# Two FFN layers behind forgetting attention: block products for w_out in the second layer's last three sets, accumulated in PSUM

## The chip, the cores and the metric

The kernel runs on one core of a Trainium2 chip. The metric is device time in microseconds (us) for one launch; "before" is the median of three runs. One further execution was recorded by the hardware profiler, and all rows below are from that one. Engines are called PE (TensorE: matmul), PEld (its weight loads, which overlap PE), DVE (VectorE), ACT (ScalarE), POOL (GpSimd) and SP (SyncE, which issues most DMAs).

## The reference, cut to what matters

```python
x = attention(q, k, v, f)                  # -> 2304 tokens x 512
for w_in, w_out, bend in ((moe_w_in, moe_w_out, lambda h: h - np.tanh(h)),
                          (moe2_w_in, moe2_w_out, lambda h: h / (1.0 + np.exp(-h)))):
    h = x @ w_in                           # 512 -> 2048
    x = bend(h) @ w_out                    # 2048 -> 512
```

The weights arrive as float64 and are decoded on the chip. Every matmul operand is kept as a high and a low float32r part, so one product of two matrices is three matmuls: high times high, high times low, low times high.

## The kernel before

The feed-forward part is cut into 24 units `u`: layer `l` (2), set `s` of 512 hidden columns (4), block `b` of 768 tokens (3). The change begins at unit 15, so layer 2 (`l` = 1), set 1, and covers units 15 to 23.

**w_in.** A set has two pairs `q` of 256 hidden columns. For each pair a slot (two slots in a unit) forms the hidden block by seven block products (`product`, line 417) in place of eight: the block of x (two halves of the 512 inputs by two halves of 384 tokens) and the block of w_in enter as sums and differences. A block product is two halves of the contraction times three terms, six matmuls of 384 columns. Each goes to a PSUM bank of its own (`ps_h`, four banks). DVE adds the banks up in SBUF (`add`, line 470), ACT applies the bend (line 447), and ACT and DVE make the high and the low part `gh`, `gl` of the bent block (lines 456 and 460). The seven sums of x, split into high and low, lie in DRAM (`xd`) and are loaded again for each unit (`xload`, line 290, 768 KB each).

**w_out.** `project` (line 385) multiplies plainly. In layer 2 the bent block is the stationary operand and w_out the moving one: a unit takes 72 matmuls of 512 columns, in 16 "halves" that a slot's list of pieces (`P1 G P6 G P2 G G P7 G P5 G P4 G P3 G`, P a product, G a half) puts between the products of the next unit. They add up in two pairs of banks (`ps_a`), and DVE adds them into `x` (line 401) or, in the last set, into `ob`, which is stored (line 405). The last half uses 256 columns (line 367).

**Weights.** A decode of one pair is: load raw (line 146), `scale` on ACT (155), `shift`, `exponent`, `low`, `join` on DVE (159, 163, 166, 174), four block sums on DVE for w_in (179), then the high part on ACT (191) and the low part on DVE (193). `fills` deals these jobs to slots; w_out is only joined and split. The scratch tiles are `wa`, `wb` and `ws`.

The whole order is written out by hand: each engine executes its instructions in program order.

Of the kernel before, what the change touches and what calls it, by code (L numbers as in the profile page):

```python
# [14 lines left out]
P = 128  # L15
# [22 lines left out]
KA = {1: 1, 2: 2, 3: 6, 4: 0, 5: 3, 6: 4, 7: 5}  # L38
# [3 lines left out]
def forgetting_attention_two_ffn(  # L42
# [16 lines left out]
    rawp = ctx.enter_context(tc.tile_pool(name="rawp", bufs=2))  # L59
# [68 lines left out]
    def open_pools(bank=None, **bufs):  # L128
        for name, n in bufs.items():
            pools[name] = ctx.enter_context(tc.tile_pool(name=name, bufs=n, reuse_waits="tile"))  # L130
        if bank:
            name, n = bank
            pools[name] = ctx.enter_context(tc.tile_pool(name=name, bufs=n, space=PSUM, reuse_waits="tile"))

    raws, wtiles, wjobs = {}, {}, {}
    ODD_FIRST = (1, 0)

    def wload(q, m, parts=(0, 1)):
        if q >= 2 * NPR:
            return  # L140
        l, c = divmod(2 * q, NFC)
        if (q, m) not in raws:
            raws[q, m] = rawp.tile([P, 2, DM, 2], U32, tag="raw", name=f"raw{q}_{m}")
        for i in parts:
            to = raws[q, m][:, i].rearrange("p n w -> p (n w)")
            nc.sync.dma_start(out=to, in_=(w_in, w_out)[m][l][c + ODD_FIRST[i]])

    def wjob(q, m, what, part=None):

        st = wjobs.setdefault((q, m), {})  # L150
        i = slice(0, 2) if part is None else slice(part, part + 1)
        n = f"{q}_{m}"
        if what == "scale":
            high = rd(raws[q, m][:, i, :, 1])
            nc.scalar.activation(high, high, AF.Prelu, scale=2.0 ** -112, alpha=-(2.0 ** 32))
        elif what == "shift":
            if "a" not in st:
                st["a"] = wtmp.tile([P, 2, DM], U32, tag="wa", name=f"wa{n}")
            nc.vector.tensor_scalar(st["a"][:, i], raws[q, m][:, i, :, 1], 3, None, ALU.logical_shift_left)
        elif what == "exponent":  # L160
            if "b" not in st:
                st["b"] = wtmp.tile([P, 2, DM], F32, tag="wb", name=f"wb{n}")
            nc.vector.tensor_scalar(st["b"][:, i].bitcast(U32), st["a"][:, i], 0xFF800000, None, ALU.bitwise_and)
        elif what == "low":
            b = st["b"][:, i]
            nc.vector.scalar_tensor_tensor(b, raws[q, m][:, i, :, 0], 2.0 ** -52, b, ALU.mult, ALU.mult)
        elif what == "join":
            if "w" not in st:
                if m == 0:
                    st["s"] = wtmp.tile([P, 8, 256], F32, tag="ws", name=f"ws{n}")  # L170
                    st["w"] = st["s"][:, 0:4].rearrange("p (i k) f -> p i (k f)", i=2)
                else:
                    st["w"] = rd(st["a"])
            nc.vector.tensor_tensor(st["w"][:, i], rd(st["a"][:, i]), st["b"][:, i], ALU.add)
        elif what == "sum":
            s = st["s"]
            to, p, op, r = ((4, 0, ALU.add, 1), (6, 2, ALU.subtract, 0),
                            (5, 4, ALU.subtract, 2), (7, 3, ALU.subtract, 5))[part]
            nc.vector.tensor_tensor(s[:, to], s[:, p], s[:, r], op)
        else:  # L180
            if (q, m) not in wtiles:
                shape = [P, 8 if q % NSLOT < 2 else 7, 256] if m == 0 else [P, 2, DM]
                wtiles[q, m] = [
                    wpool[q % NSLOT, m].tile(shape, F32R, tag=f"w{s}{q % NSLOT}_{m}", name=f"w{s}{n}") for s in "hl"
                ]
            hi, lo = wtiles[q, m]
            frm = st["s"][:, 1:8] if m == 0 else st["w"]
            c = i if m else (slice(0, 3), slice(3, 7), slice(7, 8))[part]
            frm = st["s"][:, 0:1] if m == 0 and part == 2 else frm[:, c]
            if what == "hi":  # L190
                nc.scalar.copy(hi[:, c], frm)
            else:
                nc.vector.tensor_tensor(lo[:, c], frm, rd(hi[:, c]), ALU.subtract)  # L193

# [11 lines left out]
    for s in range(2 * NSET):  # L206
# [36 lines left out]
        for d, js in plan.items():  # L243
            fills.setdefault(k + d, []).extend(js)
        late.add(k + 7)
        fills.setdefault(k + 7, []).extend(jobs(o, 1, LAST))
# [65 lines left out]
    for u, (l, s, b) in enumerate(units):  # L312
# [30 lines left out]
    halves = [(u, h, q, i, g) for u in range(len(units)) for h in range(2) for q in range(2)  # L343
              for i in (1, 0) for g in range(2)]
    halves[-16:] = sorted(halves[-16:], key=lambda t: (t[1], t[4]))
    FINAL = halves[-1][:2] + (1,)
    gfree, gt, accs, hs = list(range(4)), {}, {}, {}

    def project(n):
# [4 lines left out]
        woh, wol = (w[:, i] for w in wtiles[2 * (u // NB) + j, 1])  # L354
        first, last = j == 0 and i == 1, j == 1 and i == 0
        if first and (u, h, g) == FINAL:
            accs[u, h, g] = [pools["ps_h"].tile([P, 512], F32, tag="h", name=f"a{u}_{h}_{k}") for k in range(2)]
        elif first:
            accs[u, h, g] = pools["ps_a"].tile([P, 2, 512], F32, tag="a", name=f"a{u}_{h}_{g}")
        acc = accs[u, h, g]  # L360
        ks = range(2) if l == 0 or g == 0 else range(1)
        if (u, h, g) == FINAL:
            for k in range(2):
                c = slice(256 * k, 256 * k + 256)
                js = slice(2 * P, 3 * P)
                for r, (w, m) in enumerate(((gh, woh), (gh, wol), (gl, woh))):
                    nc.tensor.matmul(acc[k][:, 0:256], w[:, i, js], m[:, c], start=first and r == 0, stop=last and r == 2)  # L367
            if not last:
                return
            ob = wtmp.tile([P, DM], F32, tag="wa", name=f"ob{u}_{h}_{g}")  # L370
            for k, queue in enumerate((nc.scalar, nc.sync)):
                c = slice(256 * k, 256 * k + 256)
                nc.vector.tensor_tensor(ob[:, c], acc[k][:, 0:256], x[:, 2 * h + k, NT - 256:NT], ALU.add)
                queue.dma_start(out=out[NT - P:NT, c], in_=ob[:, c])
            return
# [10 lines left out]
        if g == 1 and i == 0 and (u, h) != (len(units) - 1, 1):  # L386
            gfree.append(slot)
        if not last:
            return
        del accs[u, h, g]  # L390
# [9 lines left out]
        elif l == 0 or s + 1 < NSET:  # L400
            nc.vector.tensor_tensor(total, acc, total, ALU.add)  # L401
        else:
            ob = wtmp.tile([P, 2, DM], F32, tag=("wb", "wa")[g], name=f"ob{u}_{h}_{g}")
            ob = ob[:, 0:2 - g]
            nc.vector.tensor_tensor(ob.rearrange("p t (k w) -> p k t w", w=256), acc, total, ALU.add)
            t0 += 256 * g
            nc.sync.dma_start(out=out[t0:t0 + P * (2 - g), :].rearrange("(t p) d -> p t d", p=P), in_=ob)

    def product(u, j, i):
        q = 2 * (u // NB) + j  # L410
        wih, wil = (w[:, KA[i]] for w in wtiles[q, 0])
        xh, xl = xo[u, i][:, 0], xo[u, i][:, 1]
        dst = pools["ps_h"].tile([P, 512], F32, tag="h", name=f"h{u}_{j}_{i}")[:, 0:TH]
# [6 lines left out]
    def plain(u, j, r, h, k):  # L420
        q = 2 * (u // NB) + j
        c = ((1, 2), (7, 0))[r][k]
        wih, wil = (w[:, c] for w in wtiles[q, 0])
        xh, xl = (xo[u, ((1, 7), (2, 3))[k][h]][:, e] for e in range(2))
        if k == 0:
            hs[h, r] = pools["ps_h"].tile([P, 512], F32, tag="h", name=f"h{u}_{j}_{h}_{r}")[:, 0:TH]
# [45 lines left out]
    def slot_steps(sl):  # L472
# [7 lines left out]
        elif sl == NSL - 1:  # L480
            pieces = "P1 G P6 G P2 G G P7 G P5 G P4 P3 G G".split()
# [7 lines left out]
        for p, what in enumerate(pieces):  # L489
            if what == "G":  # L490
                if n0 + g >= 0:
# [11 lines left out]
            else:  # L503
# [21 lines left out]
                else:  # L525
# [5 lines left out]
                    if sl == NSL - 1:  # L531
                        rest()
            for fn, a in xplan.get((sl, p), []):
                fn(*a)
            for job in todo[slice(*share.get(p, (0, 0)))]:
                fill(job)
            yield

# [387 lines left out]
    with tc.manual_schedule():  # L926
        slots = [slot_steps(sl) for sl in range(NSL)]
# [6 lines left out]
        rest()  # L934
        for n in range(8 * (NSL - 2) + 2, len(halves)):
            project(n)
# [39 lines left out]
```

## Time and profile before

| | |
|---|---|
| median of 3 runs | 936.65 us (936.59 to 937.1) |
| span of the profiled execution (first to last instruction) | 934.7 us |
| median less span | 1.95 us |
| PE busy | 927.5 us, 5532 matmuls |
| DVE busy | 729.9 us |
| ACT busy | 438.5 us |
| slot 30 (unit 15) begins at | 633.9 us |

The profiled execution has no time of its own beside its span; the 1.95 us are taken to lie around the span. Busy time is an average over stages with different limits. Matmuls overlap in the pipe, so what one costs is the distance from its start to the next one's, not its length in the row. The same holds for two instructions that follow each other on DVE.

### The profile page before, as it was taken

To read this page: it belongs to the slowest core of one execution; us is meant where nothing else is said; L and a number is where in the kernel's file an instruction comes from. 1 tells how busy PE (TensorE), PEld (TensorE's weight loads), DVE (VectorE), ACT (ScalarE), POOL (GpSimd) and SP (SyncE) were. 2 spreads that over 40 slices of the span, in tenths; PEclk is the share of its full clock that TensorE was granted. 3 is DMA by queue.
4 is the path that set the end of the run, shared out by engine and by line. 5 is a ranking of instruction groups with operands and counts; after the bars stand their busy time and mean duration, and the time that the engine had idled before them with its cause. 6 is when DMAs were issued, how large, how long until landed. Compare 5 with 4: busy or idle time off the path is not lost.

```text
span 934.7 us, 14918 instructions
## 1 busy us (share of the span) xinstructions
PE 927.5 (99%) x5532; PEld 846.4 (91%) x5532; DVE 729.9 (78%) x1320; ACT 438.5 (47%) x790; POOL 174.3 (19%) x248
## 2 busy tenths in 40 slices
PE   8999999999999999999999999999999999999998
PEld 6777777799999999999999999988888989888887
DVE  7798998899887887888788988877776677664444
ACT  6889888666353424242424354645342334232311
POOL 8999999300000000000000011010000000000000
PEclk9999999999999999999999999999999999999999
DMA  5434442657556764675477337564875477436722
GB/s 162 151 97 174 139 154 63 259 238 318 207 204 272 280 199 144 268 279 187 160 264 280 144 140 281 181 257 171 326 268 189 166 265 253 144 126 231 253 85 102
DMA packets 45946, 188.89 MB, mean 202 GB/s; under 512 B 9456, under 2 KB 9712, under 8 KB 45840
## 3 DMA queue, kind: packets, MB, share of 16 engines
q1 hardware_dynamic: 45720, 187.77, 55.2%
q8 instruction: 44, 0.72, 0.3%
q14 instruction: 30, 0.25, 0.1%
q10 hardware_dynamic: 152, 0.15, 0.1%
HBM read 148.44 MB, written 38.34 MB: 200 GB/s over the span
## 4 chain that ended last, share of the span: by engine, by line
PE 98%; POOL 1%; DVE 1%; issue 0%; ACT 0%; POOLq 0%
PE a L385 42%; PE h L417 34%; PE t L707 5%; PE s L660 5%; PE out_t L763 4%; PE h L431 3%; PE s L652 2%; PE out_t L791 1%; PE out L763 0%; PE a L367 0%; POOL p L695 0%; DVE wl L193 0%; DVE xt L267 0%; POOL de L783 0%; ACT gh L456 0%
## 5 line engine op out<-in xcount | busy, mean ns | idle before, releaser
L417 PE MATMUL h<-xo,wh 128*128 128x384 f32 x1232 | 313.8, 335 | 0.0
L470 DVE TENSOR_TENSOR hs<-h,hs 128x384 f32<-128x384 f32 x308 | 170.6, 554 | 90.0 <-PE h L417 86.2
L417 PEld LDWEIGHTS h<-xo,wh 128*128 128x128 f32 x1232 | 225.4, 188 | 14.1
L447 ACT ACTIVATE t<-hs 128x768 f32<-128x768 f32 x88 | 74.6, 847 | 309.3 <-DVE hs L470 309.3
L417 PE MATMUL h<-xo,wl 128*128 128x384 f32 x616 | 206.8, 336 | 0.0
L385 PE MATMUL a<-gh,wh 128*128 128x384 f32 x384 | 128.4, 334 | 0.0
L385 PE MATMUL a<-gl,wh 128*128 128x384 f32 x384 | 128.3, 334 | 0.0
L385 PE MATMUL a<-gh,wl 128*128 128x384 f32 x384 | 128.3, 334 | 0.0
L460 DVE TENSOR_TENSOR gl<-t,gh 128x768 fp32r<-128x768 f32 x96 | 91.5, 953 | 33.2 <-ACT gh L456 32.9
L417 PEld LDWEIGHTS h<-xo,wl 128*128 128x128 f32 x616 | 115.6, 188 | 0.0
L385 PE MATMUL a<-wh,gl 128*128 128x512 f32 x284 | 112.6, 396 | 0.0
L385 PE MATMUL a<-wl,gh 128*128 128x512 f32 x284 | 112.2, 395 | 0.0
L385 PE MATMUL a<-wh,gh 128*128 128x512 f32 x284 | 110.5, 389 | 0.0
L456 ACT CAST gh<-t 128x768 fp32r<-128x768 f32 x96 | 80.4, 837 | 33.4 <-DVE t L449 27.9
L281 POOL TENSOR_TENSOR xo<-xt,xo 128x768 fp32r<-128x768 f32 x3 | 6.2, 2069 | 425.8 <-ACT xo L280 425.8
L681 ACT ACTIVATE p<-p,mn 128x128 f32<-128x128 f32 (+3 forms) x128 | 71.2, 559 | 17.3 <-DVE mn L673 14.6
L695 POOL TENSOR_SCALAR p<-p,sm 128x128 f32<-128x128 f32 (+3 forms) x128 | 72.9, 588 | 7.2 <-DVE sm L692 6.7
L385 PEld LDWEIGHTS a<-gh,wh 128*128 128x128 f32 x384 | 72.1, 188 | 0.3 <-DVE x L401 0.3
L385 PEld LDWEIGHTS a<-gh,wl 128*128 128x128 f32 x384 | 72.1, 188 | 0.0
L385 PEld LDWEIGHTS a<-gl,wh 128*128 128x128 f32 x384 | 72.1, 188 | 0.0
L673 DVE CUSTOM_DVE_ANT_0 p<-s,mask 128x128 f32<-128x128 f32 (+3 forms) x128 | 59.5, 478 | 13.8 <-PE s L660 13.8
L401 DVE TENSOR_TENSOR x<-a,x 128x768 f32<-128x768 f32 (+2 forms) x60 | 57.0, 951 | 9.2 <-PE a L385 9.1
(104 smaller groups left out, 1392.1 us busy)
## 6 DMA issues: line engine op xcount, KB each, us to landing
xo<-xd SPq DMA_DIRECT2D x126, 768.0 KB
xd<-xo SPq DMA_DIRECT2D x42, 768.0 KB
raw<-w_in SPq DMA_DIRECT2D x32, 512.0 KB
raw<-w_out SPq DMA_DIRECT2D x32, 512.0 KB
kqraw<-kq SPq DMA_DIRECT2D x16, 608.0 KB
vraw<-v SPq DMA_DIRECT2D x16, 320.0 KB
out<-ob SPq DMA_DIRECT2D x6, 512.0 KB
out<-ob SPq DMA_DIRECT2D x5, 256.0 KB
```

Of the source, the lines that this page charges most:

```text
L385: nc.tensor.matmul(dst, w, m, start=first and r == 0, stop=last and r == 2)
L401: nc.vector.tensor_tensor(total, acc, total, ALU.add)
L417: nc.tensor.matmul(dst, w[:, ks], m[:, k], start=k == 0 and r == 0, stop=k == 1 and r == 2)
L447: nc.scalar.activation(t, hs[h], AF.Silu if l else AF.Tanh)
L456: nc.scalar.copy(gh, hs[h])
L460: nc.vector.tensor_tensor(gl, hs[h], rd(gh), ALU.subtract)
L470: nc.vector.tensor_tensor(to, p, s, ALU.add)
L660: nc.tensor.matmul(s[:, h, c:c + n], a[half(h), q], b[half(h), 0:n], start=r == 0, stop=r == 3,)
L673: nc.vector.tensor_tensor_reduce(out=pt.rearrange("p (g c) -> p g c", g=2) if i == 4 else pt, in0=src, in1=m, op0=ALU.add, op1=ALU.min, sc ...
L681: nc.scalar.activation(pt, pt, AF.Exp, bias=mn, scale=-1.0, accum_out=sums[:, n // 3 % 5, n % 3, 0:1],)
L695: nc.gpsimd.tensor_scalar(pt, pt, sm[:, j:j + 1], 1.0, ALU.mult, ALU.mult)
L707: nc.tensor.transpose(t[:, k], pt[:, c * P:c * P + P], ident)
```

## The change

From unit 15 on the slot machinery stops, and `joint()` writes the rest. Its unit has 14 steps on PE, alternating a w_in step of this unit with a w_out step of the unit before.

- A w_in step (`h_step`) is one block product for both pairs (12 matmuls of 384 columns, the same number as before). The sums are kept in PSUM: of two double banks `y` and `z`, products 1, 6, 7, 4 add into `y`; ACT copies `y` into `z` twice in between, and 2 and 3 add onto the copies; 5 starts `z` afresh.
- A w_out step (`c_step`) is one of seven block products with w_out: 18 matmuls of 256 columns, seven steps to a unit in place of the 72 matmuls of 512 columns. Its sums are chained the same way, with three ACT copies `seed`, and DVE adds the finished quarters into `x` (`gain`).
- The sums of the bent block are made by DVE (`two`), and each is split by ACT and DVE into a ring of three tiles (`gtile`). w_out's blocks get four sums on DVE in each decode, as w_in's do; the three blocks beyond four lie in the freed tiles of `gp0` and `gp1` (`extra`). `joint` decodes set 1's two w_out pairs over steps 0 to 16 of its first units, all but the end of three more pairs over steps 16 to 40, and the rest in the same pattern during set 2.
- x's sums are loaded into a ring of three tiles, three products ahead (`ring_load`), in place of seven tiles.
- All eight PSUM banks are given out anew as four double banks (`open_banks`).
- The order of `joint()` is made by `planned`: a list of tasks with a due time, an engine and a length in steps of 2080 ns is sorted into one program order by simulating the engines. PE's tasks keep their order. Decode parts have no `keen` mark; copies, gates and gains have it.
- In the last unit the steps are ordered `1 5 6 2 7 3 4`, and the four quarters are stored as they become ready.

```diff
+U0 = 15
+S0 = U0 // 3
...
+    RECIPE = (
+        ((7, 0, PLUS, 1), (6, 2, MINUS, 0), (4, 7, MINUS, 2), (5, 3, MINUS, 4)),
+        ((6, 0, MINUS, 2), (5, 1, MINUS, 0), (4, 1, MINUS, 6), (7, 3, MINUS, 4)),
+    )
...
+        if s == S0 - 1:
+            last_in = {4: jobs(e, 0, HILO) + jobs(o, 0, SCALING, PRE), 5: jobs(o, 0, SUMS, HILO)}
+            plan = {d: js for d, js in plan.items() if d < 4} | last_in
+            plan[3] = [j for j in plan[3] if j[1] == 0]
...
+            accs[u, h, g] = bank("a", g) if u == U0 - 1 else pools["ps_a"].tile(
+                [P, 2, 512], F32, tag="a", name=f"a{u}_{h}_{g}")
...
-                if n0 + g >= 0:
+                if 0 <= n0 + g < 16 * (U0 - 1):
                     project(n0 + g)
...
+    STEPS = (1, 2, 6, 3, 7, 5, 4)
...
+    def chain(u):
+        return bank("h", u % 2), bank("h", 1 - u % 2)
+    def h_step(u, k):
+        i, l = STEPS[k], units[u][0]
+        y, z = chain(u)
+        dst = z if i in (2, 3, 5) else y
+        t = ring.pop((u, i))
+        for j in range(2):
+            wih, wil = (w[:, KA[i]] for w in wtile(2 * (u // NB) + j, 0))
+            for d in range(2):
+                ds = slice(d * P, d * P + P)
+                for r, (w, m) in enumerate(((wih, t[:, 0]), (wih, t[:, 1]), (wil, t[:, 0]))):
+                    nc.tensor.matmul(
+                        dst[:, j, 0:TH], w[:, ds], m[:, d], start=i in (1, 5) and d == r == 0,
+                        stop=d == 1 and r == 2, skip_group_check=True,
+                    )
+        ring_load(7 * (u - U0) + k + 3)
...
+    def csteps(u):
+        return STEPS if u < LASTU else (1, 5, 6, 2, 7, 3, 4)
+    def c_step(u, k):
+        l, i = units[u][0], csteps(u)[k]
+        acc, fresh = cbank(u, i)
+        t = gtile(7 * u + k)
...
+        for d in range(3 if l else 2):
+            ds = slice(d * P, d * P + P)
+            for j, (wh, wl) in enumerate(ws):
+                gh, gl = (t[:, e, j] for e in range(2))
+                if l:
+                    dst = acc[:, d // 2, 256 * (d % 2):256 * (d % 2) + 256]
+                    terms = ((gh[:, ds], wh), (gh[:, ds], wl), (gl[:, ds], wh))
...
+        base = {u: steps * (u - U0) for u in range(U0, len(units) + 1)}
...
+            if g == S0:
+                a, b = list(decode(e - 2, 1, 0)), list(decode(o - 2, 1, 0))
+                at = [(t + 2, a[-2]), (t + 10.5, b[-4]), (t + 14, b[-2])]
+                parts = a + b
+                t0, t1 = t, t + 16
...
+            if e < 2 * NPR:
+                a, b, c = list(decode(e, 0, 0)), list(decode(e, 1, 0)), list(decode(o, 0, 0))[:-2]
+                at = t + 36.2
+                parts = a + b + c
+                spread(t + 16, t + 40, [((at,) if j is c[-2] else ()) + j for j in parts])
...
+                for k, i in enumerate(STEPS):
+                    kd = kz if i in (2, 3, 5) else ky
+                    r = [kd] + [wkey(q + j, 0, k // 4) for j in range(2)]
+                    task(t0 + 2 * k, "P", 1, lambda u=u, k=k: h_step(u, k), r, (kd,))
...
+                cp(t0 + 1.05, zs, ys, kz, ky)
+                gate(t0 + 3.05, g1, zs, f1, kz)
+                cp(t0 + 5.05, zs, ys, kz, ky)
+                cp(t0 + 7.05, g12, zs, f12, kz)
+                cp(t0 + 9.05, g22, ys, f22, ky)
+                two(t0 + 11.05, g22, zs, g22, PLUS, f22, kz, f22)
+                two(t0 + 11.5, g12, zs, g12, PLUS, f12, kz, f12)
+                gate(t0 + 11.55, g22, g22, f22, f22)
+                gate(t0 + 12.0, g12, g12, f12, f12)
+                if l:
+                    two(t0 + 12.5, ta, g12, g22, PLUS, fa, f12, f22, False)
+                    two(t0 + 12.7, g12, g1, g12, MINUS, f12, f1, f12, False)
+                    two(t0 + 12.9, tb, ta, g1, MINUS, fb, fa, f1, False)
...
+                gate(t0 + 13.15, g21, ys, f21, ky)
+                two(t0 + 15.3, g21, g21, tb, MINUS, f21, f21, fb, False)
...
+                when = {k: 10 + 2 * k for k in range(7)}
+                when[1], when[2] = 14.0, 14.5
...
+                    task(t0 + when[k], "A", N2, lambda g=g, f=frm: copy(g[:, 0], f), (kf,), (("gh", kg),))
+                    task(t0 + when[k] + 0.1, "V", W2, lambda g=g, f=frm: tt_(g[:, 1], f, rd(g[:, 0]), MINUS),
+                         (kf, ("gh", kg)), (("gl", kg),))
...
+            if not first and 3 * (v // NB) == 3 * S0 and S0 % NSET:
+                task(t0 + 3, "V", W2, lambda a=xs[12], b=xs[22]: tt_(a, a, b, MINUS), (kx[12], kx[22]), (kx[12],))
+            if not last:
+                seed(t0 + 2.05)
+                gain(t0 + 4.05, 11, zs, kz, copies=first)
+                send(t0 + 4.6, 11)
+                seed(t0 + 6.05)
+                gain(t0 + 8.05, 12, zs, kz, copies=first)
+                seed(t0 + 10.05)
+                gain(t0 + 10.45, 12, ys, ky, MINUS)
+                gain(t0 + 12.05, 22, zs, kz, copies=first)
+                if s == NSET - 1:
+                    task(t0 + 12.5, "V", W2, lambda a=xs[12], b=xs[22]: tt_(a, a, b, PLUS), (kx[12], kx[22]), (kx[12],))
...
+                gain(t0 + 14.05, 21, ys, ky, copies=first)
...
-        slots = [slot_steps(sl) for sl in range(NSL)]
+        slots = [slot_steps(sl) for sl in range(2 * U0)]
...
-        rest()
-        for n in range(8 * (NSL - 2) + 2, len(halves)):
-            project(n)
+        open_banks()
+        joint()
```

## Rows read from the trace of the kernel before

**Rows 1.** The page, its busy times (us, share of the span, instructions) by engine.
```profile
PE 927.5 (99%) x5532; PEld 846.4 (91%) x5532; DVE 729.9 (78%) x1320; ACT 438.5 (47%) x790; POOL 174.3 (19%) x248
```
**Rows 2.** Chain that ended last, by line, from 640 us on.
```profile
by line: PE a L385 54.0%; PE h L417 44.0%; PE a L367 0.9%; DVE ob L373 0.3%; issue 0.0%
```
**Rows 3.** The same chain in order of time: start, us, what.
```profile
655.00 2.08 PE a L385 x9
...
670.72 2.08 PE a L385 x9
...
912.90 2.10 PE h L417 x12
915.00 13.64 PE a L385 x60
```
**Rows 4.** Timeline at the end: first and last of 24 matmuls of 256 columns.
```profile
928.48 0.28 PE L367 MATMUL a<-wh,gh 128*128 128x256 f32 x1
...
931.24 0.28 PE L367 MATMUL a<-wh,gl 128*128 128x256 f32 x1
```
**Rows 5.** Groups of DVE instructions with shapes, 633.9 to 931.6 us: count, busy, mean ns.
```profile
L460 DVE TENSOR_TENSOR gl<-t,gh 128x768 fp32r<-128x768 f32 x38 | 36.3, 954 | 20.7 <-ACT gh L456 20.7
L401 DVE TENSOR_TENSOR x<-a,x 128x1024 f32<-128x1024 f32 x12 | 14.7, 1224 | 6.3 <-PE a L385 6.2
L166 DVE SCALAR_TENSOR_TENSOR wb<-raw,wb 128x1024 f32<-128x1024 uint32 x10 | 12.2, 1223 | 0.2
L401 DVE TENSOR_TENSOR x<-a,x 128x512 f32<-128x512 f32 x12 | 8.2, 680 | 0.0
L179 DVE TENSOR_TENSOR ws<-ws 128x256 f32<-128x256 f32 x20 | 7.8, 417 | 0.1
L163 DVE TENSOR_SCALAR wb<-wa 128x1024 uint32<-128x1024 uint32 x9 | 6.2, 685 | 0.0
L159 DVE TENSOR_SCALAR wa<-raw 128x1024 uint32<-128x1024 uint32 x9 | 6.2, 684 | 1.9 <-ACT raw L155 1.9
L174 DVE TENSOR_TENSOR ws<-wa,wb 128x1024 f32<-128x1024 f32 x5 | 6.1, 1221 | 0.1
```
**Rows 6.** Timeline of DVE: a 768-element instruction and the next one's start.
```profile
665.28 0.95 DVE L460 TENSOR_TENSOR gl<-t,gh 128x768 fp32r<-128x768 f32 x1
666.15 1.22 DVE L174 TENSOR_TENSOR ws<-wa,wb 128x1024 f32<-128x1024 f32 x1
```
**Rows 7.** Windows: PE, PEld, DVE, ACT, POOL busy, clock, DMA share, GB/s.
```profile
187.00:210.00 23.00, 23.00 (x134) 23.00 (x133) 21.65 (x29) 14.55 (x22) 0.00 (x0) 1.00 0.59 240
...
586.60:602.30 15.70, 15.70 (x80) 14.11 (x79) 14.11 (x21) 7.86 (x11) 0.00 (x0) 1.00 0.61 206
...
655.00:670.70 15.70, 15.70 (x79) 14.11 (x79) 11.71 (x18) 7.54 (x10) 0.00 (x0) 1.00 1.01 414
```
**Rows 8.** Groups of ACT instructions with shapes, 633.9 to 931.6 us.
```profile
L447 ACT ACTIVATE t<-hs 128x768 f32<-128x768 f32 x37 | 31.3, 847 | 163.5 <-DVE hs L470 163.5
L456 ACT CAST gh<-t 128x768 fp32r<-128x768 f32 x37 | 30.9, 836 | 0.5
L155 ACT ACTIVATE raw<-raw 128x1024 f32<-128x1024 f32 x9 | 10.2, 1129 | 0.0
L507 ACT COPY hs<-h 128x384 f32<-128x384 f32 x18 | 8.6, 475 | 3.8 <-PE h L417 3.5
L191 ACT CAST wh<-ws 128x1024 fp32r<-128x1024 f32 x5 | 5.2, 1049 | 8.7 <-DVE ws L179 8.7
```
**Rows 9.** Timeline around 666 us: product 1's last matmul, and ACT's copy of it.
```profile
666.20 0.33 PE L417 MATMUL h<-xo,wl 128*128 128x384 f32 x1
666.37 0.39 PE L385 MATMUL a<-wh,gh 128*128 128x512 f32 x1
666.57 0.48 ACT L507 COPY hs<-h 128x384 f32<-128x384 f32 x1 [0.32 <-PE h L417]
```
**Rows 10.** Timeline of DVE around 620 us: the wait for a high part.
```profile
620.84 0.96 DVE L460 TENSOR_TENSOR gl<-t,gh 128x768 fp32r<-128x768 f32 x1 [0.54 <-ACT gh L456]
```

More of the change, by code (lines that the diff above doesn't have):

```diff
@@ L353, in project @@
         gh, gl, slot = gt[u, j, h]
-        woh, wol = (w[:, i] for w in wtiles[2 * (u // NB) + j, 1])
+        woh, wol = (w[:, 2 * i:2 * i + 2].rearrange("p k f -> p (k f)") for w in wtile(2 * (u // NB) + j, 1))
         first, last = j == 0 and i == 1, j == 1 and i == 0
[L356 to L359, printed above, removed]
+        if first:
+            accs[u, h, g] = bank("a", g) if u == U0 - 1 else pools["ps_a"].tile(
+                [P, 2, 512], F32, tag="a", name=f"a{u}_{h}_{g}")
         acc = accs[u, h, g]
         ks = range(2) if l == 0 or g == 0 else range(1)
[L362 to L375, printed above, removed]
         for k in ks:
@@ L385, in project, with gather @@
                 nc.tensor.matmul(dst, w, m, start=first and r == 0, stop=last and r == 2)
-        if g == 1 and i == 0 and (u, h) != (len(units) - 1, 1):
+        if g == 1 and i == 0:
             gfree.append(slot)
-        if not last:
-            return
-        del accs[u, h, g]
+        if last and evac:
+            gather(n)
+    def gather(n):
+        u, h, j, i, g = halves[n]
+        l, s, b = units[u]
+        acc = accs.pop((u, h, g))
         t0 = TB * b + TH * h
@@ new lines, in planned, with ready @@
+    def planned(tasks):
+        LAG = 0.1
+        tasks = sorted(tasks, key=lambda t: t[0])
+        writer, readers, deps = {}, {}, []
+        for n, (when, eng, cost, fn, reads, writes, keen) in enumerate(tasks):
+            d = {writer[k] for k in reads if k in writer}
+            for k in writes:
+                d |= readers.pop(k, set())
+                if k in writer:
+                    d.add(writer[k])
+            d.discard(n)
+            deps.append(d)
+            for k in reads:
+                readers.setdefault(k, set()).add(n)
+            for k in writes:
+                writer[k] = n
+        free, end, order = dict.fromkeys("PAVS", 0.0), {}, []
+        queue = {e: [n for n, t in enumerate(tasks) if t[1] == e] for e in free}
+        def ready(n):
+            if all(d in end for d in deps[n]):
+                e = tasks[n][1]
+                return max([end[d] + LAG * (tasks[d][1] != e) for d in deps[n]] + [tasks[n][0] - 3])
+        while any(queue.values()):
+            best = None
+            for e, waiting in queue.items():
+                known = [(max(r, free[e]), n) for n in waiting[:1 if e in "PS" else 60] if (r := ready(n)) is not None]
+                if not known:
+                    continue
+                t = min(known)[0]
+                now = [n for r, n in known if r <= t]
+                n = min(now, key=lambda n: tasks[n][0])
+                if not tasks[n][6] and tasks[n][0] > t - 2:
+                    soon = [r for r, k in known if tasks[k][6] and t < r < t + tasks[n][2] - 0.2]
+                    if soon:
+                        t = min(soon)
+                        n = min((k for r, k in known if r <= t and tasks[k][6]), key=lambda n: tasks[n][0])
+                if best is None or t < best[0]:
+                    best = t, e, n
+            t, e, n = best
+            queue[e].remove(n)
+            free[e] = end[n] = t + tasks[n][2]
+            order.append((t, e != "P", len(order), n))
+        return [tasks[n][3] for *_, n in sorted(order)]
```

329 lines of the change are left out of this document (288 added, 41 removed).

## The prediction, made before the changed kernel was run

> **What bounds the kernel now.** The page comes first: PE is busy for 99% of the span, DVE for 78%, ACT for 47% [rows 1]. An average over stages does not decide it, so the chain that ended last comes next, from 640 us on: it consists of matmuls, with no step of "issue" worth a tenth of a per cent and one of DVE at the very end [rows 2]. So in the stretch that the change rewrites, PE never waits, and time is PE's instructions times their pace. A change here gains what it takes from PE, less the waits that it brings.
>
> The chain in order of time gives the pace [rows 3]. A slot's block of nine 512-column matmuls takes 2.08 us, 0.231 us each, and the same block comes again 15.72 us later, so a unit (two slots) takes 31.44 us. Of this the 72 matmuls of w_out are 72 x 0.231 = 16.64 us, and the 84 of w_in are the other 14.80 us, 0.176 us each (12 in 2.10 us near the end, 0.175). At the end, where only w_out's products run, 60 of 512 columns take 13.64 us, 0.2273 each. The last 24, of 256 columns, start 2.76 us apart from first to last [rows 4], so 2.76 / 23 = 0.120 us each.
>
> **What PE loses and gains.** w_in's 84 matmuls of 384 columns stay: 14.80 us a unit. w_out's 72 x 0.231 = 16.64 us become 7 x 18 = 126 matmuls of 256 columns. Their pace is the term that counts. The last 24 of this trace have exactly this form, an operand of 128x128 loaded for each, 0.120 us apart. But the 512-column ones are 0.2311 / 0.2273 = 1.017 slower in the mixed stretch than at the end; I take the same ratio, 0.122 us. So 126 x 0.122 = 15.37 us, a gain of 1.27 us a unit, and 9 units give 11.4 us. Bounds: at 0.120 it is 15.12 us, 1.52 x 9 = 13.7 us; with the whole 3.8 ns of the mixed stretch added to each matmul, 0.1238, it is 15.60 us, 1.04 x 9 = 9.4 us. The saving is an eighth of the columns (36864 to 32256); the larger count of matmuls takes back nearly 40% of what the columns alone would give.
>
> The Trainium skill prices a warm back-to-back matmul at N / 2.4 ns plus 2.5 ns (page "TensorE: Matmul & The Clock Gate", section "Back-to-back issue gap"), which is 109 ns for 256 columns and 216 ns for 512; the trace has 120 and 227, some 13 ns above the columns where the page has 2.5. By the page the sum would be 72 x 0.2158 - 126 x 0.1092 = 1.78 us a unit, 16.0 us in all; the measured pace decides.
>
> **DVE.** Per unit the new stretch has, of 768 elements each, 6 `two`, 7 low parts and 5 gains (in `joint`'s list), and one more pass over x in sets 1 and 3: 18 or 19. Such an instruction lasts 0.95 us [rows 5], but the next one that needs nothing of it starts 0.87 us after it [rows 6]. So 18 x 0.87 = 15.7 us, or 16.5. A decode is, from the mean rows [rows 5]: 0.68 + 0.69 + 1.22 + 1.22 + four sums of 0.33 to 0.42 (together about 1.5) + low parts of 1.22 and 0.95 less overlap (2.1) = 7.4 us. Set 1 carries most of them. Unit 15's 14 steps: 13 x 0.87 = 11.3, four adds of the old kind 2 x (1.22 + 0.68) = 3.8, one left-over low part 0.95, and 14/16 of two decodes, 13.0: 29.0 us, against PE's 14.80 + 16.64 = 31.4. Unit 16's: 16.5 + 1.9 + half of 21.4 (2.9 decodes over 24 steps) = 29.1 us against 14.80 + 15.37 = 30.2, so 96%. Unit 17's: 16.5 + 10.7 + 0.5 = 27.7, 92%. Set 2 falls to 25 to 27 us a unit and set 3 to 17. The trace shows DVE at 21.65 of 23 us, 94%, with PE busy all the time, and at 14.11 of 15.7, 90% [rows 7]. At 94% set 1 (85.8 us of DVE) takes 91.3 us, within PE's 91.8; at 90% it takes 95.3, 3.5 us over. So I put 1 us of waits here, bounds 0 and 3.5.
>
> **ACT and the chains in PSUM.** Per unit ACT has 18 instructions of 768 elements (4 copies in the w_in chain, 4 bends, 7 high parts, 3 seeds), at 0.84 us 15.1 us, and at most 1.4 decodes of 1.13 + 1.05 + 0.84 = 3.0 us: 19.3 of 30.2 us [rows 8]. A copy from PSUM to PSUM is not in the trace; from PSUM it is 0.475 us at 384 elements, and 384 more at the slope of SBUF casts, (1.049 - 0.836) / 256 ns, make 0.80. I take 0.85, with 0.8 and 0.95 (twice the 384 row) as ends. Five of these copies a unit stand directly between two steps on PE: `cp` at 1.05 and 5.05, `seed` at 2.05, 6.05 and 10.05. Each is covered by one step of the other product, 12 x 0.176 = 2.11 or 18 x 0.122 = 2.20 us. ACT starts on a product 0.37 us after the start of its last matmul, which is 0.20 us after the next matmul began [rows 9]. With 0.85 us of copy and 0.1 for the way back, PE can go on 1.15 us after the next step began: 0.95 us to spare. An ACT instruction just begun, at most 1.13 us (`scale`) [rows 8], makes 2.28, so a late copy costs 0.1 to 0.2 us. Therefore the steady stretch gets 0.5 us, bounds 0 and 45 x 0.1 = 4.5. The other hand-offs have more: a g tile is made 5 steps ahead, except the one of g21, whose way (two bends, five DVE instructions, split) has some 3 us to spare.
>
> **The ends.** At the start two halves of unit 14 move behind the switch, a shift of 2.1 us and no cost; the new banks must first be emptied by DVE, and unit 14's second pair of sums waits for the gathers (1.22 + 0.68 us) behind one w_in step of 2.11 us: 0.5 us, bounds 0 and 1.5. In the last unit seven w_out steps run alone, 7 x 18 x 0.120 = 15.1 us, while DVE has about 5 low parts, 2 sums and 9 gains or parts of gains, 14 us, some waiting for one another: 1 us, bounds 0 and 3. After the last matmul, one add and a store, as now.
>
> **DMA** costs nothing: the same 7 loads of 768 KB a unit, each issued when its ring tile is free, five steps or some 10.7 us before its use. The trace moves 414 GB/s at full share [rows 7], so 786 KB take 1.9 us, and a raw load of 1 MB in front of it on SP's queue 2.5 us. The cover ends if a raw load, which waits on SP for DVE's `low`, is over 5 us late; then `h_step` is next.
>
> **Sum.** 934.7 - 11.4 + 1 + 0.5 + 0.5 + 1 = 926.3 us of span, and 1.95 us outside it: 928.2 us for the median. With every bound at its best, 936.65 - 13.7 = 923.0; with 9.4 gained and 8 us of waits of a possible 12.5 (they share their causes), 935.2.
>
> **The rivals.** First, *DVE sets the time in set 1 and the last unit*: it is already at 92 to 96% there, decode parts with an early due time go ahead of gates and gains, and DVE works in program order. Waits of 3.5 + 3 and 1 + 0.5 elsewhere make 936.65 - 11.4 + 8 = 933.2. For it speaks the 90% stretch; against it the 94% one, with PE busy through both [rows 7].
>
> Second, on the other side, *the copies between steps come late at every hand-off*. There are 45 such copies, so 11.4 / 45 = 0.25 us of wait at each undoes the gain. That is reached when the copy is held back by 1.2 us, just above one ACT instruction. If one cast of 0.84 us and one of 1.05 us stand ahead each time, a hand-off takes 1.15 + 1.89 = 3.04 us, 0.9 over its cover, 40 us in all: 965 us. With 0.6 us over, 952. For it: ACT stands two thirds used and runs in order. Against it: the due times put few instructions ahead, and 0.95 us are to spare.
> The trace has DVE idle for 0.54 us before a low part while it waits for the high one [rows 10], as an engine does that keeps its order. The Trainium skill says so as a rule (page "TensorE: Matmul & The Clock Gate", the specification table: the queues of ScalarE and VectorE are strict FIFO); by it a held copy also holds what stands behind it.
>
> Third, *the pace of short matmuls follows the columns alone*: half of 0.231 us is 0.1156, 126 x 0.1156 = 14.56 us, 2.08 x 9 = 18.7 us gained, 921 us with 3 us of waits. The 0.120 of the last 24 speaks against it [rows 4].
>
> **How the numbers follow.** Forecast 0.70 (923 to 931.5, its own range); DVE setting the time 0.12 (931.5 to 935); the copies late 0.14 (above 935: 0.04 below 938.5, 0.10 beyond); columns alone 0.04. Below 923 lie 0.04 and above 934.5 about 0.15, so the range is 923 to 934.5. A measurement can tell 0.2%, 1.9 us, from no change: faster (below 934.8) has 0.70 + 0.04 + 0.11 of the second case, 0.85; same 0.05, slower 0.10.
>
> **What would show it.** In the changed profile: 256-column matmuls 0.120 to 0.124 us apart inside a step; a unit of 30.1 to 30.4 us in sets 2 and 3; PE's idle time under 4 us after the switch, most of it in units 15 to 17 and in the last unit; DVE above 90% in set 1. I am wrong if PE's share of the chain there falls below 95%, if ACT copies `z` from `y` more than 2.1 us after the step before, or if the 256-column pace is above 0.126.

## The result, and the profile after

The changed kernel takes 923.39 us (median of 4 runs, 923.27 to 923.67) where the kernel before took 936.62 in the same comparison: a ratio of 0.9858, 95% interval 0.9844 to 0.9872. That is 13.2 us saved where 8.4 were forecast. The forecast's mechanism holds; two of its prices and its waits were put too high and the end too low, and the measured time lies just inside the lower edge of the range (923.0).

The page of the changed kernel: span, then busy us, share and instructions of each engine.

```profile
span 921.4 us, 15985 instructions
PE 911.8 (99%) x6006; PEld 857.4 (93%) x6006; DVE 764.8 (83%) x1326; ACT 505.2 (55%) x871; POOL 174.0 (19%) x248
```

Against [rows 1] PE is busy for 15.7 us less, with 474 matmuls more. The chain of the changed kernel in order of time shows the pace (start, us, what); one whole unit lies between the first row and the last.

```profile
714.99 2.09 PE h L634 x12
717.08 2.19 PE a L675 x18
719.27 2.08 PE h L634 x12
721.35 2.15 PE a L675 x18
...
744.67 2.09 PE h L634 x12
```

A unit takes 744.67 - 714.99 = 29.68 us, against 31.44 before [rows 3] and 30.17 forecast. A w_out step of 18 matmuls is 2.15 us (0.1194 each), one in each unit 2.19; a w_in step of 12 is 2.08 to 2.09 us (0.174 each). So 1.76 us are saved in a unit. The seven w_out steps take 6 x 2.15 + 2.19 = 15.09 us, which leaves 14.59 for w_in: 0.21 us of the saving is w_in's, where nothing was forecast.

PE's waits from 640 us on, all that the list of waits has (us in total, times, the longest):

```profile
PEld h L634 <- ACT h L804: 0.7, 1, 0.7
PE h L634 <- ACT h L804: 0.3, 1, 0.3
PEld a L675 <- ACT a L870: 0.3, 1, 0.3
```

This is one wait at 646.6 us, in the first unit of the new stage, where a copy `z` from `y` stands behind the high part of a weight and a `scale`, and one small wait at a seed. Together they cost some 0.7 us. Four windows of the changed kernel, each about a unit; the columns are those of [rows 7]:

```profile
663.60:693.40 29.80, 29.80 (x210) 29.45 (x209) 24.64 (x31) 18.53 (x24) 0.00 (x0) 1.00 0.65 221
693.40:723.00 29.60, 29.60 (x212) 29.51 (x211) 28.25 (x38) 19.96 (x25) 0.00 (x0) 1.00 0.74 258
...
782.40:812.00 29.60, 29.60 (x211) 29.51 (x211) 27.56 (x36) 19.97 (x26) 0.00 (x0) 1.00 0.60 193
841.70:871.40 29.70, 29.70 (x213) 29.61 (x212) 17.28 (x20) 15.27 (x20) 0.00 (x0) 1.00 0.63 198
```

DVE reaches 28.25 of 29.60 us, 95%, and PE fills the same window whole. The end, by the timeline:

```profile
916.47 0.28 PE L675 MATMUL a<-weh,gr 128*128 128x256 f32 x1
...
916.79 1.09 DVE L878 TENSOR_TENSOR x<-a,x 128x256 f32<-128x256 f32 x3 [0.28 <-PE a L675]
917.58 0.43 ACTq L702 DMA_DIRECT2D out<-x  x1
917.90 0.34 SPq L702 DMA_DIRECT2D out<-x  x1
```

From the start of the last matmul to the end of the span are 921.4 - 916.47 = 4.9 us. Before they were 934.7 - 931.24 = 3.5 us [rows 4], with the last store issued at 932.00:

```profile
932.00 0.33 SPq L374 DMA_DIRECT2D out<-ob  x1
```

**The account.** Eight units, 16 to 23, mix both new kinds of step (unit 15 still carries 512-column blocks of the old kind): 8 x 1.76 = 14.1 us. The last unit's w_out steps run alone and save 72 x 0.2273 - 126 x 0.120 = 1.25 us. Less 0.7 us of waits and 1.4 us at the end, that is 13.2 us; the spans differ by 934.7 - 921.4 = 13.3 us.

### The profile page after: what moved, and what is told of

It is laid out like the page before. It is cut to its first block, busy times and chain, and to the rows that moved or that the text cites. A ratio compares the mean times of both kernels' runs of the same rounds, so it can differ in the third digit from the quotient of the medians.

```text
span 921.4 us, 15985 instructions
## 1 busy us (share of the span) xinstructions
PE 911.8 (99%) x6006; PEld 857.4 (93%) x6006; DVE 764.8 (83%) x1326; ACT 505.2 (55%) x871; POOL 174.0 (19%) x248
## 4 chain that ended last, share of the span: by engine, by line
PE 95%; DVE 2%; ACT 1%; issue 1%; POOL 0%; DMA 0%; DVEq 0%; POOLq 0%
PE a L427 26%; PE h L457 20%; PE a L675 14%; PE h L634 14%; PE t L1139 5%; PE s L1092 5%; PE out_t L1195 4%; PE h L471 3%; PE s L1084 2%; PE h L675 0%; PE out L1195 0%; PE out_t L1223 0%; ACT gh L496 0%; POOL p L1127 0%; DMA de<-x 0%
## 5 line engine op out<-in xcount | busy, mean ns | idle before, releaser
L457 PE MATMUL h<-xo,wh 128*128 128x384 f32 x728 | 185.0, 334 | 0.0
L457 PEld LDWEIGHTS h<-xo,wh 128*128 128x128 f32 x728 | 132.0, 188 | 2.6
L634 PE MATMUL h<-xr,wh 128*128 128x384 f32 x504 | 128.5, 335 | 0.3 <-ACT h L804 0.3
L510 DVE TENSOR_TENSOR hs<-h,hs 128x384 f32<-128x384 f32 x182 | 100.6, 553 | 26.7 <-PE h L457 23.8
L457 PE MATMUL h<-xo,wl 128*128 128x384 f32 x364 | 121.8, 335 | 0.0
L634 PEld LDWEIGHTS h<-xr,wh 128*128 128x128 f32 x504 | 88.5, 189 | 1.4 <-ACT h L804 0.7
L634 PE MATMUL h<-xr,wl 128*128 128x384 f32 x252 | 84.4, 335 | 0.0
L675 PE MATMUL a<-wh,gr 128*128 128x256 f32 x420 | 80.7, 282 | 0.0
L500 DVE TENSOR_TENSOR gl<-t,gh 128x768 fp32r<-128x768 f32 x60 | 57.1, 952 | 14.1 <-ACT gh L496 13.9
L457 PEld LDWEIGHTS h<-xo,wl 128*128 128x128 f32 x364 | 68.3, 188 | 0.0
```

The lines of the kernel that those rows point to most:

```text
L457: nc.tensor.matmul(dst, w[:, ks], m[:, k], start=k == 0 and r == 0, stop=k == 1 and r == 2)
L500: nc.vector.tensor_tensor(gl, hs[h], rd(gh), ALU.subtract)
L510: nc.vector.tensor_tensor(to, p, s, ALU.add)
L634: nc.tensor.matmul(dst[:, j, 0:TH], w[:, ds], m[:, d], start=i in (1, 5) and d == r == 0, stop=d == 1 and r == 2, skip_group_check=True,)
L675: nc.tensor.matmul(dst, w, m, start=fresh and (l == 0 or d != 1) and j == r == 0, stop=j == 1 and r == 2, skip_group_check=True,)
```

## The experiments

The theory at the start: the gain is a constant sum per unit of PE's pace, and copies and DVE have room. The rivals: the copies are close to their limit everywhere, DVE is just within it, or the gain comes from something that happens once.

**Fewer units.** The switch comes three and six units later, with the weights' jobs ahead of it dealt to match.

```diff
-U0 = 15
+U0 = 18        # start21: 21
```

> The new part begins at unit 18 in place of 15, so six units are rewritten in place of nine. Theory A (the gain is 1.76 us for each unit, from the two products' pace on PE, 31.44 to 29.68 us, less about 2.5 us once, at the switch and at the end): 936.6 - 6 x 1.76 + 2.5 = 928.5 us. Rival (the gain of 13.2 us is spread evenly, with nothing lost once): 936.6 - 8.8 = 927.8 us. Rival (set 1, where VectorE is fullest, gives less than the other sets): above 929 us is against it, 927 us or less for it.

> The new part begins at unit 21: three units, the last set alone. Theory A (1.76 us for each unit less 2.5 us once): 936.6 - 5.3 + 2.5 = 933.8 us. Rival (spread evenly, nothing lost once): 932.2 us.

Nine units: 923.39 us. Six: 929.66 (ratio 0.9926, 0.9909 to 0.9943). Three: 934.71 (ratio 0.998, 0.9971 to 0.9989); there the last unit subtracts a quarter of x that already holds a product, so its sums differ, and its instructions do not. So the step from three units to six is worth 5.05 us, 1.68 a unit, and the step from six to nine 6.27. Against 1.76 us a unit, the kernels with nine, six and three units fall short by 2.6, 3.6 and 3.4 us. The gain goes by units, with a nearly fixed sum lost once, as the theory has it; both times came out about 1 us above its forecasts (928.5 and 933.8), because the sum is larger in the two shorter kernels. Both wait at their own switch 0.8 us for DVE's `x` in a w_out block, which the nine-unit kernel does not. The rival in which set 1 gives less would have needed 927 us or less with six units.

**Every copy between banks two and three times.** The copies are ACT's `cp` (18) and `seed` (25).

```diff
-task(when, "A", N2, lambda to=zs, frm=ys: copy(to, frm), (ky,), (kz,), True)
+task(when, "A", N2, lambda to=zs, frm=ys: [copy(to, frm) for _ in range(2)], (ky,), (kz,), True)
```

> Each of the 43 copies in PSUM between two steps is issued twice, 0.75 us more on ScalarE for each hand-off; the result is the same. Theory (a hand-off takes about 1.1 us and has some 1 us to spare under the other product's step of 2.1 us): under 3 us slower than the changed kernel, 923.4 to 926.4 us, with waits only where ScalarE has another instruction ahead. Rival (the hand-offs are near their edge): 0.5 us for each of 43, 945 us.

> Each of the 43 copies is issued three times, 1.5 us more for each hand-off. Theory (1 us to spare): PE waits some 0.45 us at each, 43 x 0.45 = 19 us, 943 us, and up to 955 us, since ScalarE then is busy for 26 of 30 us of a unit. Rival (the copies lie beside other waits and cost nothing even so): under 928 us.

Measured: 935.59 us with two and 961.44 us with three, one run each: 12.2 and 38 us above the changed kernel. The theory's "under 3 us" fell: 935.59 lies between it and the rival's 945, and 961 us is above all that was expected of three. The list of waits, first of the doubled kernel, then of the tripled one:

```profile
PEld a L675 <- ACT a L870: 12.8, 19, 1.1
PE a L675 <- ACT a L870: 7.0, 17, 0.8
PE h L634 <- ACT h L804: 0.9, 1, 0.9
```

```profile
PEld a L675 <- ACT a L870: 27.8, 25, 1.9
PE a L675 <- ACT a L870: 20.1, 19, 1.6
PEld h L634 <- ACT h L804: 11.9, 18, 1.4
```

Doubled, nearly all of the loss stands at seeds (line 870; 19 times, 12.8 us of late weight loads), while the 18 `cp` (line 804) cost PE one wait. Tripled, all 18 `cp` cost one too. So the copies do not all have the same room: a `cp` has room for one more copy but not for two, and many seeds not for one. The timeline of the changed kernel says why. ACT at a second and a third seed, then DVE at the third:

```profile
795.47 0.84 ACT L839 CAST gr<-f_a 128x768 fp32r<-128x768 f32 x1 [1.19 <-PE a L675]
796.21 0.80 ACT L870 COPY a<-a 128x768 f32<-128x768 f32 x1
...
803.94 0.83 ACT L839 CAST gr<-f 128x768 fp32r<-128x768 f32 x1 [0.20 <-PE a L675]
805.05 0.78 ACT L870 COPY a<-a 128x768 f32<-128x768 f32 x1 [0.27 <-DVE x L878]
```

```profile
804.06 0.95 DVE L878 TENSOR_TENSOR x<-x,a 128x768 f32<-128x768 f32 x1 [1.21 <-PE a L675]
```

The second seed stands behind a high part that became free at the same moment, and ends 0.47 us before the next w_out step (797.48). The third stands behind a high part and behind DVE's subtraction, which reads the bank that the seed copies; it ends at 805.83, and the next w_out step begins at 805.95. It has nothing to spare. The Trainium skill has a rule that fits this last wait (page "PSUM — Partial Sum Buffer", section "PSUM bank collisions raise a hardware error"): the compiler orders any two instructions on different engines that touch the same bank and quadrant, reads included. The trace agrees: DVE's read ends at 805.01 and ACT's copy begins at 805.05. The third seed is also what makes one w_out step of each unit 2.19 us and not 2.15.

**The doubled copies with the seeds put first.** The high parts are due a little after the seed, and the subtraction waits for the third seed.

```diff
-when = {k: 10 + 2 * k for k in range(7)}
-when[1], when[2] = 14.0, 14.5
+when = {k: 10.2 + 2 * k for k in range(7)}
+when[1], when[2] = 14.2, 14.5
...
-gain(t0 + 10.45, 12, ys, ky, MINUS)
+gain(t0 + 10.45, 12, ys, ky, MINUS, after=(kz,))
```

> The doubled copies again (935.6 us), with two changes of order: the seeds of w_out's chain go ahead of the high part that becomes free at the same moment, and the subtraction from y that VectorE makes goes behind the third seed. Theory (copies and seeds themselves have 1 us to spare; the 12 us of the doubled run are lost at the seeds, which stand behind a cast of 0.84 us and, the third, behind VectorE's read of the same bank): under 926.5 us, with PE waiting for seeds under 2 us in all. Rival (each hand-off has only some 0.5 us to spare, wherever it stands): 934 to 936 us.

Measured: 925.23 us, one run: 10.4 us of the 12.2 are back, with all 43 copies still doubled. Its list of waits:

```profile
PEld a L675 <- ACT a L870: 1.8, 4, 0.7
PE a L675 <- ACT a L870: 0.8, 3, 0.3
PEld h L634 <- ACT h L804: 1.9, 2, 1.5
```

So the cost was the place in ACT's order and the shared bank, not ACT's time. The two edits were made together; what each is worth alone was not measured.

**DVE's margin.** Each low part is computed twice, 7 x 0.87 = 6.1 us more of DVE in a unit; the order of the program is planned as for one.

```diff
-lambda g=g, f=frm: tt_(g[:, 1], f, rd(g[:, 0]), MINUS)
+lambda g=g, f=frm: [tt_(g[:, 1], f, rd(g[:, 0]), MINUS) for _ in range(2)]
```

> Each low part of the bent block is computed twice, 7 x 0.87 = 6.1 us more of VectorE in a unit; the result is the same. Theory (VectorE is the next limit: 23 to 28 us busy of 29.7 in sets 1 and 2, so units 15 to 20 come to 25, 31, 34, 30, 32 and 34 us): 13 to 16 us slower than the changed kernel, 936 to 940 us, all of it in sets 1 and 2. Rival (the low parts have five steps of room, so VectorE is not next): under 927 us. Rival (VectorE's order already held PE up, as the DVE case of the prediction has it): over 945 us.

Measured: 951.21 us, one run, 28 us above the changed kernel where 13 to 16 were expected. The number lies in the last rival's range, but its reason does not hold: the changed kernel's list has no wait of PE for DVE. Windows of this kernel, with the columns of [rows 7] (the granted clock is the third from the end):

```profile
663.60:694.00 30.40, 29.46 (x207) 29.06 (x206) 29.76 (x37) 18.05 (x25) 0.00 (x0) 1.00 0.60 213
694.00:726.00 32.00, 26.15 (x178) 25.63 (x177) 31.31 (x40) 16.05 (x20) 0.00 (x0) 0.95 0.67 236
...
823.00:853.00 30.00, 27.27 (x179) 26.95 (x180) 26.68 (x33) 16.42 (x22) 0.00 (x0) 0.91 0.39 132
...
722.60:729.40 6.80, 5.16 (x22) 5.16 (x23) 5.62 (x6) 4.88 (x7) 0.00 (x0) 0.50 0.07 28
821.60:828.30 6.70, 3.80 (x18) 3.80 (x18) 5.62 (x7) 4.96 (x7) 0.00 (x0) 0.50 0.10 42
```

and its longest waits of PE:

```profile
PE a L675 <- ACT a L870: 16.4, 7, 5.5
PE a L675 <- DVE x L878: 2.1, 1, 2.1
```

and PE's timeline after a long wait:

```profile
724.24 0.58 PE L675 MATMUL a<-weh,gr 128*128 128x256 f32 x1 [5.17 <-ACT a L870]
...
728.25 0.84 PE L634 MATMUL h<-xr,wh 128*128 128x384 f32 x2
...
730.87 0.28 PE L675 MATMUL a<-weh,gr 128*128 128x256 f32 x1
```

DVE is indeed the next limit: it is busy for 98% of the window in which PE loses most (31.31 of 32.00). Its share alone does not decide, though: between 823 and 853 us PE waits with DVE at 89%. The price has three parts. First, the waits, in few, long pieces of up to 5.5 us: by the starts of matmuls, against those of the changed kernel, the 13 longest gaps hold 22.4 us (the list has 21, since it counts from a matmul's modelled end). In the chain from 704 to 724 us DVE does decode parts (`wa`, `wb`, `ws`) between the low parts that PE needs, in an order planned for shorter ones. Second, the granted clock is at its lower level (0.50, so 1.2 of 2.4 GHz) in two stretches, each of which begins while PE stands in a wait of over 5 us. After the wait that ends at 724.24, a w_out step takes 4.01 us in place of 2.15 and the w_in step behind it 2.62 in place of 2.09, with no wait in either; after the one that ends at 824.50 a w_out step takes 3.96. That is 1.86 + 0.53 + 1.81 = 4.2 us. The rest, some 1.5 us, is in shorter gaps.

**What slows the 512-column matmuls beside others.** The kernel before had 0.2311 us for them in the mixed stretch and 0.2273 alone. If each change between the two products costs something, longer blocks help. The kernel before, with its layer-2 pieces in longer blocks:

```diff
-P1 G P6 G P2 G G P7 G P5 G P4 G P3 G
+P1 P6 P2 P7 G G G G P5 P4 P3 G G G G      (quads)
+P1 P6 G G P2 P7 G G P5 P4 G G P3 G G      (pairs)
```

> The kernel before, with one list changed: in the second layer's slots (but the first and the last) four products stand together, then four halves, three products, four halves, in place of one or two of each in turn. The matmuls are the same. Theory (the 512-column halves and the 384-column products cost each other some 0.03 us at each change from one to the other, seven pairs of changes a slot): with two pairs 5 x 0.04 to 0.06 us less a slot, 22 slots, 3 to 6 us faster than before, 930.5 to 933.5 us. Rival (the pace of 0.231 and 0.176 us belongs to the matmuls and not to their turns): within 0.5 us of 936.6. Rival (the products' sums are then taken late and PE waits): slower.

> The kernel before, with the second layer's slots (but the first and the last) in the order two products, two halves, so four pairs of changes between products and halves in a slot in place of seven. Theory (0.06 us for a pair of changes between 384 and 512 columns; two halves in a row already occur without a wait): 22 slots x 3 x 0.06 = 4.0 us faster than before, 932 to 933.5 us. Rival (the pace belongs to the matmuls): 936.6 us. Rival (sums taken late, as with four in a row): slower, with waits of PE for VectorE.

Measured: quads 987.28 us (ratio 1.0537, 1.0521 to 1.0552), pairs 939.88 us (ratio 1.0035, 1.0022 to 1.0048); both are misses. Quads lost its time to waits (`a` here is w_out's sums, `x` DVE's add of them):

```profile
PEld a L385 <- DVE x L401: 32.4, 20, 5.0
PE a L385 <- DVE x L401: 24.1, 13, 4.7
```

Pairs lost 3.2 us, of which 2.2 are waits of PE for DVE's and ACT's reads of w_out's sums, as the last rival had it. Its pace says more. Its chain in order of time:

```profile
706.52 2.08 PE a L385 x9
708.61 2.10 PE h L417 x12
...
722.23 2.08 PE a L385 x9
```

A slot takes 722.23 - 706.52 = 15.71 us with 8 changes in it, as it did with 15.72 and 14 [rows 3]. A fixed price for each change is ruled out.

The place in a block does count, and quads shows it. The first and the tenth 512-column matmul of a block of 18, with products before and behind, and the first product after it:

```profile
709.58 0.39 PE L385 MATMUL a<-wh,gh 128*128 128x512 f32 x1
...
711.66 0.39 PE L385 MATMUL a<-wh,gh 128*128 128x512 f32 x1
...
713.70 0.51 PE L417 MATMUL h<-xo,wh 128*128 128x384 f32 x2
```

The first nine start 2.08 / 9 = 0.231 us apart, the other nine 2.04 / 9 = 0.227. The 60 in a row at the end of the kernel before fit this: 9 x 0.231 + 51 x 0.2267 = 13.64 us [rows 3]. So 0.231 is the pace of the first nine behind a block of products, and pairs, with blocks of nine, could not get below it. The products do likewise: quads' blocks of 24 take 4.17 to 4.20 us, 0.174 to 0.175 each, though they too stand beside 512 columns.

**Only the width changed.** The kernel before, with each 512-column matmul of layer 2 cut into two of 256: same columns, same order, same banks.

```diff
+if l:
+    for e in range(2):
+        es = slice(256 * e, 256 * e + 256)
+        for r, (w, m) in enumerate(terms):
+            nc.tensor.matmul(dst[:, es], w, m[:, es], start=first and r == e == 0, stop=last and r == 2, skip_group_check=True)
```

> The kernel before, with each 512-column matmul of the second layer's w_out cut into two of 256 columns on the same operand: 144 in place of 72 a unit, none saved by block products. The result is the same. Theory (256 columns take 0.1195 us also between 384-column products, and the products then keep 0.174 us): a unit takes 144 x 0.1195 + 84 x 0.1742 = 31.84 us in place of 31.44, for 12 units 4.8 us slower, 941.4 us. Rival (the pace that I predicted, 0.122 and 0.1762): 32.37 us a unit, 11 us slower, 947.8 us.

Measured: 940.64 us (ratio 1.0042, 1.0028 to 1.0056). The chain of this kernel:

```profile
703.66 2.15 PE a L388 x18
705.81 1.04 PE h L423 x6
706.85 1.43 PE a L388 x12
...
719.53 2.15 PE a L388 x18
```

Eighteen of 256 columns take 2.15 us and six of 384 take 1.04 us (0.174): the changed kernel's two paces, in the old order and without its chains, copies or longer steps. In blocks of this length the pace goes with the width (and, with it, the doubled number of weight loads): behind 256 columns w_in's products run at 0.174, behind 512 at 0.176, and 256-column matmuls behind products are no slower than the 0.120 of a long run.

**The end and the seeds.** First, only the end: the last product's third quarter is issued last, and one sum of quarters comes earlier.

> The end alone: the last w_out step is issued as tokens 0 to 255 first and the other 128 behind them, with the first two adds between; and the upper-right quarter takes in the lower-right one before its own last product, not after. Theory (the changed kernel ends 4.9 us after its last matmul's start where the one before took 3.5, because three adds and 768 KB of stores stand behind the last matmul; now one add and 128 KB do): 1.2 to 1.5 us less than the changed kernel, 921.9 to 922.2 us, and the last matmul is again some 3.5 us from the end. Rival (the store's landing sets the end, whatever stands ahead of it): within 0.3 us of 923.4.

Measured: 923.45 us (ratio 0.9857, 0.9841 to 0.9874), no gain: the rival's number, though the last run below, which gains at this end, speaks against its reason. The timeline shows that all three adds still wait for the last matmul; they read one double bank:

```profile
916.77 1.09 DVE L881 TENSOR_TENSOR x<-a,x 128x256 f32<-128x256 f32 x3 [0.51 <-PE a L675]
```

So the last third goes into the spare double bank, the subtraction from that quarter is moved ahead of the last product, and the seeds are put first as above.

```diff
-task(when, "P", 1, lambda v=v, k=k: c_step(v, k), r, (kd,))
+if last and k == 6:
+    task(when, "P", 0.667, lambda v=v, k=k: c_step(v, k, (0, 1)), r, (kd,))
+    task(when + 0.01, "P", 0.333, lambda v=v, k=k: c_step(v, k, (2,), chain(v)[1]), r[1:], (("h", 1 - v % 2),))
...
-gain(t0 + 5.5, 12, ys, ky, MINUS)
+gain(t0 + 5.5, 21, csum(v, y, 2), ky, d=2)
```

> The changed kernel with the seeds put first, and with another end: the last step's last 128 tokens go to a bank of their own, so that the two adds for the others no longer wait for them; what y held for these tokens is added before; the upper-right quarter takes in the lower-right one in the steps before, which drops one pass of VectorE. Theory (the first try at the end gained nothing because the adds still waited for the whole double bank): 1.0 to 1.5 us less than the changed kernel at the end and up to 0.3 at the third seeds, 921.7 to 922.4 us. Rival (the landing of the stores sets the end): 923.1 to 923.5 us.

> The kernel of the run before with the last add reading the columns that the last product writes; nothing else differs and the whole of the reference is computed. Theory (the seeds' order is worth about 0.5 us of waits and the shorter last steps about 1 us): 921.7 to 922.2 us, ratio to the kernel before 0.984 to 0.985. Rival (the add now depends on an earlier part of the spare bank and waits longer): 922.4 to 923.0 us, with a wait of the last add longer than 0.5 us in the list of waits.

The first of the two took 921.91 us (ratio 0.9842, 0.9827 to 0.9857); its last add reads 256 columns of the spare bank that the last product does not write, so one third of a quarter of the output is not the reference's. The second reads the right ones and computes all of it: 921.99 us (921.89 to 922.13; ratio 0.9844, 0.983 to 0.9857), 1.4 us below the changed kernel and the fastest whole kernel here. Its timeline:

```profile
915.78 0.76 DVE L882 TENSOR_TENSOR x<-a,x 128x256 f32<-128x256 f32 x2 [0.48 <-PE a L675]
...
916.18 0.28 PE L675 MATMUL h<-weh,gr 128*128 128x256 f32 x1
916.50 0.42 DVE L924 TENSOR_TENSOR x<-h,x 128x256 f32<-128x256 f32 x1
916.57 0.42 ACTq L702 DMA_DIRECT2D out<-x  x1
```

Two adds now lie beside the last matmuls. From the last matmul to the end are 920.3 - 916.18 = 4.1 us in place of 4.9: 0.8 us of the 1.1 by which the span fell. The other 0.3 is PE's, whose last matmul starts at 916.18 and not 916.47; no wait at a seed is left in PE's list.

## Why the prediction came out as it did

- *PE is the bound, and a change gains what it takes from PE.* Right. The unit fell by what its blocks fell by, and PE fills every window from 663.6 to 899.3 us.
- *The pace of 256 columns, 0.122 us.* Mis-sized. It was the 0.120 of the last 24 times the ratio 1.017 that 512 columns show between the mixed stretch and the end. The ratio belongs to the first nine 512-column ones behind products: narrow has 0.1194 for 256 columns between w_in's products with the old order. The steps take 15.09 us a unit where 15.37 were put, 0.28 less; the 0.120 bound (15.12) was the better value.
- *"w_in's 84 matmuls of 384 columns stay: 14.80 us a unit."* Failed by 0.21 us a unit, in the same direction: their 0.176 was the price in short blocks beside 512 columns. The first term, forecast at 11.4 us, was 15.3. The Trainium skill's formula (page "TensorE: Matmul & The Clock Gate", section "Back-to-back issue gap", there for an isolated matmul) had given 1.78 us a unit, and 1.76 was measured. That is no confirmation: each of its prices is 10 to 15 ns below the row (109 to 119 ns, 216 to 227 or 231), and the sum by it lets w_in gain nothing.
- *DVE, 1 us of waits.* None came in sets 1 to 3. The demand was over-counted: 23.25 + 24.64 + 28.25 = 76.1 us busy in set 1, not 85.8. The bound near 94% was placed well enough for this order: 95% of a window goes without a wait. It is no general share: lows2 waits at 98% and, in another window, at 89%.
- *The copies, 0.85 us each, with 0.95 us to spare at all 45.* The length was close: 0.784 us at `cp`, 0.788 at `seed` (18 and 25 in the groups, so 43 and not 45). The cost was near what was put, one wait of 0.3 us. The spare time was wrong for two of the three seeds, which have 0.47 us and about 0.1. What the step left out is that a high part becomes free with the same matmul and is ahead in ACT's order, and that DVE reads the same bank. The rival of late copies was nearer than its price said: one further copy at each hand-off costs 12 us.
- *"After the last matmul, one add and a store, as now."* Failed by 1.4 us. It is three adds, all behind the last matmul, and the last store is issued on SP's queue at 917.90, 1.4 us after that matmul's start; before it was 0.8 us (932.00 - 931.24). The rest is the stores' own time, 3.5 us to the end of the span in place of 2.7.
- *Start 0.5 us, last unit 1 us of waits.* The first wait was 0.5 us. The last unit's steps ran through.
- *DMA nothing.* Right. PE's list has no wait for a load of `xr` from 640 us on.

The forecast was 4.8 us too long: pace and neighbours +3.9, waits that did not come +2.3, the end -1.4. That the measured time lies in the range is in part luck, since these errors have opposite signs: with the end as it was put, 3.5 us, the kernel would have taken 922.0 us, below 923. Of the signs named in advance, PE's short idle time and DVE above 90% (once, 95%) came, while the unit (29.68 us) and the 256-column pace (0.1194) fell below what was named. The third rival (columns alone, 0.1156) came nearer with its 921 us than the forecast did, for a wrong reason: 0.1194 is not half of 0.231, nor of 0.2273.

What stays open is why the first nine 512-column matmuls behind 384-column ones take 0.231 us each and the later ones 0.227, why the products behind them start slowly too, and why 256-column ones do not. It is not a fixed price for each change (pairs) and not the order or the banks (narrow).

## What to carry to other kernels

When PE sets the end, price a new width of matmul by a row of that width, and price what stays at its pace beside the new neighbours: here 0.176 became 0.174 for free, and an extrapolated ratio cost more accuracy than it brought. Before a ratio of two paces is carried over, look where in a block the difference lies. For every copy that hands a PSUM bank on between two matmul blocks, write down what becomes free at the same moment on its engine and who else reads the bank; put the copy first in both orders. Look at what stands behind the last matmul by itself: here an add of one part of a double bank waited for the last matmul into any part of it.

## What the hardware showed that was not expected

- Behind 384-column matmuls the first nine of 512 columns start 0.231 us apart and the later ones 0.227; in blocks of six to twelve the 384-column ones then take 0.176. With 256 columns in their place it is 0.1194 and 0.174.
- ACT copies 768 columns from PSUM to PSUM in 0.784 to 0.788 us, less than its casts of as many from SBUF (0.835 to 0.839).
- Long waits of PE cost twice. In lows2 PE waited in pieces of up to 5.5 us, and in the two longest the granted clock fell to its lower level (0.50, 1.2 GHz of 2.4): 4.2 us of slower steps on top of 22 us of waiting.
